# Delta-rule attention and a gated MLP on one Trainium2 core: a new list for the order of all instructions

## Chip, cores and metric

The kernel runs on one core of a Trainium2 chip. The metric is the device time of one execution in microseconds (us). The engines are TensorE (PE, matmuls), VectorE (DVE), ScalarE (ACT) and GpSimd (POOL); SyncE (SP) issues all bulk transfers.

## What is computed

The reference takes `q`, `k`, `v` (4 batches, 8 heads, 768 positions, 48 features) and `beta`, and runs a delta-rule attention over the positions; the result, reshaped to 4 x 768 x 384, goes through a gated MLP. `w_in` is 384 x 1024, `w_spatial` 768 x 768, `w_out` 512 x 384.

```python
k_n = k / (norm(k, axis=-1) + 1e-06)
state = zeros((B, H, D, D))
for t in range(S):
    y[t] = q[t] @ state
    v_old = state^T k_n[t]
    state += beta[t] * outer(k_n[t], v[t] - v_old)

h = relu(x @ w_in)                # x is y, heads side by side
u, v = h[..., :512], h[..., 512:]
v_n = (v - mean(v)) / sqrt(var(v) + 1e-06)
v_s = w_spatial @ v_n + b_spatial # over the positions
out = (u * v_s) @ w_out
```

## The kernel before, in words

**Attention.** The loop over 768 positions is done in chunks of 64. Twelve chunks for each of two pairs of batches make 24 steps `s`, and four steps make a group `g` (six groups). `prep(g)` (L476) makes the products of keys of its four steps (matmuls `kk`), copies them out, transposes them (L525), works out norms (L533 to L541) and scales the matrix `la` (L543). Then it inverts small unit triangular matrices one column at a time: each column is a product and a sum on DVE, a "lane". Group 0 uses 16 x 16 blocks and DVE alone (`lanes16`, L576 and L581); the later groups use 32 x 32 blocks, with some columns on DVE and the others on POOL (`lanes`, L563 and L568). ACT copies the DVE part out of PSUM (L586, L594), and one DVE transpose (L595) brings the result into `xt`. `widen16` (L655; group 0 only) and `widen` (L621) merge the blocks to 64 x 64 by matmuls: for a pair of steps, DVE transposes the diagonal blocks into `tn` (L625), PE does `e`, ACT scales its result into `tn` (L646), PE does `f`, and ACT copies that back (L651). `step(s)` (L730) then does the recurrence of one chunk: `v` minus the old state's part (L747 on DVE into `bn`), the product with the inverse, `w` (L777 on ACT), the state's update (L790, L792 on DVE), and the output (L807 on ACT). `scale_v` (L707) and the masked product of queries and keys (L724) stand ahead of it.

**Weights.** `w_in`, `w_spatial` and `w_out` arrive as raw 64-bit floats, and `load_f64` (L386) turns them into 32-bit ones with a chain over DVE (L392, L398, L400), ACT (L394 to L397, L401) and DVE or POOL (L402, L403). `split_w` (L382) splits each into a high part (ACT, L383) and a remainder (DVE or POOL, L384: `win_l`, `wsp_l`, `wout_l`), as each matmul of the MLP is three: high x high, high x remainder, remainder x high.

**Gated MLP.** After every second step `convert` (L817) brings 128 positions of two batches into the layout of the MLP and splits them (`xh` on ACT at L827, `xl` on DVE or POOL at L828); `mlp_v`, `norm_v`, `split_v` (L880) and `mlp_u` make the two halves of `h`, `mlp_g` (L948) does the products over positions and the gate (L962, L965, L967, L968), and `mlp_o` the last product and the store. Matmuls of all parts are recorded at one line, L453.

**Order.** Nothing is issued when these functions run. They record 2642 operations in a `Plan` (L167); an operation that can run on two or three engines has them listed in `alt`. `ORDER` (L36) is a list of words; each is four times the number of an operation plus the index of the engine that it takes. `Plan.issue` (L204) goes through the list, so the list sets the order on each engine and on SP's transfer queue, the choice of engine, and which buffer of a pool an operation gets:

```python
for i, sel in order:
    o = self.ops[i]
    for p, h in o.acq:
        h.unit = self.pools[p].pop(0)
    if o.fn is not None:
        e = list(o.alt)[sel]
        o.fn(e) if len(o.alt) > 1 else o.fn()
```

Of the kernel before, what the change touches and what calls it, by code (L numbers as in the profile page):

```python
# [36 lines left out]
12 0 28 52 64 4 40 448 8 928 24 32 56 36 68 60 44 936 88 85 1076 72 1064 49  # L37
80 96 93 292 20 16 1112 100 344 452 108 152 112 116 468 1080 120 124 456 128 132 136 1100 1084
160 140 608 460 148 1068 156 144 464 296 1088 1072 164 472 396 312 1692 500 168 476 300 932 172 348
480 1696 624 612 628 484 1104 176 304 489 76 180 184 2348 1108 188 552 352 192 1092 632 616 196 696  # L40
504 356 200 621 364 204 208 360 212 216 492 220 224 692 664 1096 400 2336 228 508 497 1732 232 236
308 240 104 244 1689 248 512 252 256 1729 404 260 264 268 516 1129 272 276 280 556 668 680 672 1125
284 684 677 408 1116 944 520 708 688 572 316 712 716 948 412 940 288 416 1000 952 560 320 524 1120
368 564 420 324 720 568 528 956 724 328 1004 728 576 736 372 988 424 532 1736 993 1008 969 732 1012
332 428 536 376 432 336 740 980 580 960 380 986 1060 966 744 996 1016 973 584 976 1640 1021 1028 541
1132 1040 1644 1048 1026 1045 1652 1648 588 1034 1656 1660 384 1136 1036 748 1140 1144 1668 1148 1664 752 388 1680
1700 1152 436 1156 1160 1704 756 440 1164 1708 592 1672 2340 1054 1168 1724 1712 1189 1056 596 1980 1740 2344 1172
1676 1716 1176 760 1684 1180 764 1984 544 392 636 1184 1720 2332 1196 1296 1200 445 1192 1748 1204 1744 1208 1752
1212 1216 1308 1220 1312 1224 2029 1756 1228 1992 1760 1232 1324 1236 1328 1768 1240 1776 601 1244 1248 1772 1252 1764
1988 1340 1796 2032 1256 341 1996 1260 1784 640 652 644 2000 1264 1800 2036 1344 2040 1792 1268 1356 2004 548 1788  # L50
2008 2016 2020 2048 1272 604 1360 2360 656 2044 1372 1780 1276 1376 2052 648 2056 1280 1388 700 1284 2068 661 1288
2060 2072 1292 2076 2064 1804 2352 1300 2092 704 2012 872 2081 1304 2356 2024 2384 1316 1808 2084 2372 1320 1392 2088
1404 1332 1408 2100 2096 1420 1836 1336 1424 1348 1436 1840 1352 1440 1916 1364 1452 2104 1368 876 1920 1380 1456 880
1384 1844 1468 2108 1396 1472 1400 2120 1484 1412 1924 1416 1488 2124 1428 1500 884 1432 2144 2376 1504 1444 892 1516
2112 1448 2140 2380 1460 1520 1464 2152 1532 888 1476 2364 1536 1480 2128 2400 896 1848 2136 2368 1492 2961 1928 1496
2132 2396 1508 1932 1512 1936 900 2148 1524 1852 1548 904 1528 2964 1552 3784 1540 1944 1544 1564 1940 1556 1568 2392
1560 1812 1580 1572 1576 1584 2116 1588 909 1856 2972 1592 2452 1816 913 1948 1952 916 2389 1956 2968 1820 1608 1621
2404 1628 3016 1601 1626 1960 1604 1964 1614 1632 1824 1968 1616 1636 2912 2408 921 1597 1828 3020 2916 2156 768 2412
3012 2920 2160 2924 1832 2928 2932 2416 2976 2164 2936 2420 2940 2168 2424 1972 2428 2952 772 2980 1976 2432 2948 2436
2984 2944 2440 2444 2172 2956 2988 776 2448 2992 2461 2456 2188 3432 780 3008 2568 2580 788 2192 2996 2584 784 2196  # L60
2596 2468 2472 2600 2200 2476 792 3024 2480 2612 2464 2484 3000 2616 2488 3028 2628 3436 3004 2632 2492 2496 2204 2644
2176 796 2500 2180 2648 2504 3032 2660 2184 2508 3036 1861 2512 2208 2664 2516 2268 2676 3040 2520 2300 2680 3440 2524
3044 2692 3444 2528 3052 1868 2696 3448 3060 3048 3452 2708 2532 3056 3492 2712 2536 1864 3481 3080 3484 2540 2544 3460
3064 2304 2213 3496 3468 2308 2724 3076 3456 2548 2272 2728 3488 3472 2276 3072 1873 1876 2740 2552 800 3084 3500 2744
2556 3504 3068 1880 2560 1885 2312 2756 2564 3796 3508 3533 2572 2280 2316 2576 2284 2588 2760 2320 2592 2772 2288 2604
2328 2776 3520 3088 2608 2788 3512 2620 1889 3524 2792 2624 3528 3093 2636 2324 3800 3516 2640 3544 3820 3804 2652 2216
2656 3536 3548 2804 3464 2668 3096 2808 3540 2296 3476 3100 2220 2672 3104 2684 1892 2688 2225 3552 1896 2228 2700 1900
2232 3556 2704 2237 2716 2820 3108 2292 2720 2824 3560 2732 3120 2241 2736 805 2748 3572 2752 2764 3112 3576 2768 3124
2836 2780 809 3116 2784 3584 3824 2796 2800 3588 3128 2812 3828 2840 2816 2828 3132 2852 3848 2832 2856 2844 3788 2848
2860 3564 812 3808 2864 3136 3792 3600 817 3200 3140 3204 3832 3208 3844 3212 820 3216 3596 3220 2900 2893 3812 3592  # L70
3900 2881 3232 3604 2872 2905 3236 3580 2897 2878 3240 2885 3244 2908 3816 3248 2888 4360 3252 3224 3841 3568 4364 3608
4409 4412 4368 4420 4372 3612 3228 4376 4380 3144 4416 3837 3720 4388 3724 4424 4384 2868 1904 3852 4400 4428 3256 4432
1909 4396 3728 4436 3732 3260 3152 4712 4440 4461 4448 3856 4456 4444 3752 4452 3860 3864 3756 3148 3868 3760 3872 3764
3156 3768 3876 3160 4392 3880 3772 3164 3884 4404 4464 3169 3776 3888 4472 3173 4468 3897 3736 4476 3740 4480 3748 3744
4484 2244 3892 3904 3616 4488 3908 3916 1912 4492 4500 3176 4760 3920 3780 4508 4016 3912 3924 4028 4496 4716 4032 3928
4044 3620 3932 3181 3936 3184 4048 3640 3940 2249 3644 4504 3648 824 4724 3944 4516 4060 3652 4720 3948 4064 4528 2252
3952 4728 4772 4076 3956 4080 4512 4764 3188 3960 4092 4732 6124 4096 4768 4524 3656 4108 4740 3624 3964 3193 4736 4776
4520 3628 2256 4752 3968 3632 6112 3972 4780 3636 4532 2260 4784 3976 4112 3264 4788 3980 4124 3268 3660 3984 4128 3272
3988 828 3276 4140 3992 3280 4144 832 3284 3996 4156 840 4800 4160 3288 4744 4792 4172 4804 3292 4176 4808 4796 4536
3296 4188 3300 4192 2264 3304 4813 4824 4748 836 4816 4756 4204 3308 844 3320 848 3324 4820 852 3328 3312 857 3332  # L80
3316 3336 3340 861 4828 3376 4000 4832 3344 3665 4836 3668 4208 4004 3348 4541 4852 4008 3672 3352 4012 3356 4840 4020
3380 4024 3360 6736 4844 4036 4220 3364 4040 3677 3384 3680 4224 4052 4848 3368 3684 4056 3388 4236 864 4864 3372 3392
3396 4876 3688 4068 3404 3693 3696 4872 3408 4072 4240 3400 3412 4252 4860 3416 3701 4084 3420 4256 4088 3424 4268 4100
# [1022 lines left out]
```

## Time and profile before

| | |
|---|---|
| median of 3 runs | 447.9 us |
| the runs | 447.9, 449.64, 447.23 us |
| profiled execution, span | 449.0 us |
| PE busy | 400.4 us (89%), 8648 matmuls |
| DVE busy | 282.0 us (63%), 692 instructions |
| ACT busy | 251.0 us (56%), 548 instructions |
| POOL busy | 177.9 us (40%), 352 instructions |
| bulk transfers | 41.27 MB in 15936 packets |
| program text fetched while it runs | 68 packets, 1.11 MB |

The profile gives one execution; its span is its own time, 1.1 us above the median and inside the range of the runs. Its chain of work that ended last goes through PE for 73%, DVE for 12%, ACT for 7%, transfers for 4% and for 3% through waits that nothing in the profile ends. "Idle before" stands for the time in which the engine did nothing ahead of an instruction, and behind the arrow is what ended it.

### The profile page before, as it was taken

How to read it: one execution, taken by the hardware profiler on the slowest of the kernel's cores; microseconds unless marked ns; L12 is line 12 of the kernel's file. 1: busy time of each engine (PE TensorE's matmuls, PEld its weight loads, DVE VectorE, ACT ScalarE, POOL GpSimd, SP SyncE). 2: the span in 40 equal slices, each digit the busy share in tenths (PEclk: the TensorE clock that was granted, in tenths of full speed). 3: DMA queues.
4: the chain of work that ended last, by engine and by line, in shares of the span. 5: the costliest groups of instructions: out<-in, count | busy, mean ns of one | idle time of the engine just before them, and what ended most of it. 6: DMA issues, size and time to landing. Idle time of an engine off the chain costs nothing.

```text
span 449.0 us, 19525 instructions
## 1 busy us (share of the span) xinstructions
PE 400.4 (89%) x8648; PEld 362.6 (81%) x8648; DVE 282.0 (63%) x692; ACT 251.0 (56%) x548; POOL 177.9 (40%) x352
## 2 busy tenths in 40 slices
PE   3414577889998999999999999999999999999996
PEld 3314577678788798879889889899889899999996
DVE  2889899898967669838898789824312323441330
ACT  4789864786676663877345874255435751430212
POOL 5162176838654845322784248540312100221121
PEclk9999999999999999999999999999999999999999
DMA  7951066324443423043241230132201000000102
GB/s 251 318 209 39 3 218 208 111 70 170 141 131 109 141 85 113 9 133 117 86 153 58 86 110 19 69 112 86 92 12 38 2 35 1 19 0 37 72 35 89
DMA packets 16020, 42.51 MB, mean 95 GB/s; under 512 B 3392, under 2 KB 7616, under 8 KB 15936
## 3 DMA queue, kind: packets, MB, share of 16 engines
q1 hardware_dynamic: 15936, 41.27, 27.3%
q8 instruction: 68, 1.11, 1.0%
q14 instruction: 16, 0.13, 0.1%
HBM read 35.36 MB, written 4.72 MB: 89 GB/s over the span
## 4 chain that ended last, share of the span: by engine, by line
PE 73%; DVE 12%; ACT 7%; DMA 4%; issue 3%; SPq 0%; POOL 0%; DVEq 0%; ACTq 0%
PE ps L453 73%; DVE prod L563 2%; DVE ps L568 2%; ACT xt L327 2%; DMA vf<-in_w_in 1%; DMA g<-in_w_out 1%; DMA ke<-in_k_t 1%; DVE xt L595 1%; DVE ut L398 1%; ACT xt L651 1%; DVE ps L581 1%; ACT w L777 1%; DVE prod L576 1%; ACT tn L646 1%; DVE ut L392 1%
## 5 line engine op out<-in xcount | busy, mean ns | idle before, releaser
L453 PE MATMUL ps<-wsp_h,vf 128*128 128x256 f32 x480 | 104.1, 286 | 0.0
L453 PEld LDWEIGHTS ps<-wsp_h,vf 128*128 128x128 f32 x480 | 80.7, 188 | 1.7 <-ACT ut L904 0.3
L453 PE MATMUL ps<-wsp_l,vf 128*128 128x256 f32 x240 | 67.5, 281 | 0.0
L568 DVE TENSOR_TENSOR ps<-ps,prod 128x60 f32<-128x60 f32 (+9 forms) x150 | 45.9, 306 | 3.9
L563 DVE TENSOR_TENSOR prod<-ps,la 128x60 f32<-128x60 f32 (+9 forms) x150 | 44.7, 298 | 4.0
L453 PEld LDWEIGHTS ps<-wsp_l,vf 128*128 128x128 f32 x240 | 45.2, 188 | 0.3
L962 DVE TENSOR_TENSOR gt<-ps,bbc 128x512 f32<-128x512 f32 x18 | 12.4, 690 | 43.6 <-PE ps L453 43.6
L568 POOL TENSOR_TENSOR wl<-wl,prod 128x36 f32<-128x36 f32 (+4 forms) x90 | 32.4, 360 | 5.8
L563 POOL TENSOR_TENSOR prod<-wl,la 128x36 f32<-128x36 f32 (+4 forms) x90 | 31.5, 350 | 5.7
L453 PE MATMUL ps<-wout_h,g 128*128 128x384 f32 x112 | 30.9, 339 | 0.0
L453 PE MATMUL ps<-ke 64*64 64x64 f32 x704 | 18.3, 253 | 11.2 <-DMA ke<-in_k_t 4.6
L453 PE MATMUL ps<-bn 64*64 64x64 f32 x832 | 20.2, 241 | 8.9 <-ACT xt L327 4.5
L453 PEld LDWEIGHTS ps<-ke 64*64 64x64 f32 x704 | 15.2, 161 | 15.1 <-ACT xt L327 5.8
L453 PEld LDWEIGHTS ps<-bn 64*64 64x64 f32 x832 | 16.7, 150 | 13.0 <-ACT xt L327 5.4
L965 POOL TENSOR_TENSOR gt<-gt,ut 128x512 f32<-128x512 f32 x9 | 11.6, 1287 | 34.3 <-DVE gt L962 23.7
L453 PE MATMUL ps<-wsp_h,bn 128*128 128x256 f32 x96 | 24.9, 282 | 0.0
L724 DVE TENSOR_TENSOR pt<-ps,masks 128x512 f32<-128x512 f32 x24 | 16.4, 682 | 13.5 <-PE ps L453 13.5
L967 ACT CAST xt<-gt 128x512 fp32r<-128x512 f32 x10 | 6.2, 620 | 32.2 <-DVE gt L965 21.2
L651 ACT COPY xt<-ps 32x256 f32<-32x256 f32 x48 | 17.5, 364 | 11.1 <-PE ps L453 10.5
L968 POOL TENSOR_TENSOR xt<-gt,xt 128x512 fp32r<-128x512 f32 x5 | 6.5, 1296 | 43.3 <-ACT xt L967 35.4
L967 ACT CAST g<-gt 128x512 fp32r<-128x512 f32 x14 | 8.5, 616 | 26.4 <-DVE gt L965 16.7
L327 POOL COPY xt<-xt 32x512 f32<-32x512 f32 (+1 forms) x22 | 13.7, 623 | 22.8 <-DVE xt L595 11.2
(193 smaller groups left out, 1114.9 us busy)
## 6 DMA issues: line engine op xcount, KB each, us to landing
bn<-in_bun SPq DMA_DIRECT2D x22, 896.0 KB, 4.8
ke<-in_k_t SPq DMA_DIRECT2D x22, 256.0 KB, 4.0
out<-ob SPq DMA_DIRECT2D x24, 192.0 KB, 1.9
vf<-in_w_in SPq DMA_DIRECT2D x6, 512.0 KB, 6.7
g<-in_w_sp SPq DMA_DIRECT2D x3, 768.0 KB, 5.6
g<-in_w_out SPq DMA_DIRECT2D x4, 384.0 KB, 3.2
bn<-in_bun SPq DMA_DIRECT2D x2, 640.0 KB, 7.5
xs<-xs SPq DMA_DIRECT2D x66, 16.0 KB, 2.9
```

The costliest lines, as they stand in the source:

```text
L327: (nc.scalar.copy if e == "ACT" else ENG[e].tensor_copy)(out=out_, in_=in_)
L392: P.add({"DVE": d}, lambda: nc.vector.tensor_scalar(out=eu(), in0=w1(), scalar1=20, scalar2=0x7FF, op0=ALU.logical_shift_right, op1=ALU.bi ...
L398: P.add({"DVE": dve_t(n)}, lambda: nc.vector.scalar_tensor_tensor(out=eu(), in0=w1(), scalar=0x80000000, in1=eu(), op0=ALU.bitwise_and, op ...
L453: nc.tensor.matmul(o, l, r, start=start, stop=stop)
L563: P.add({eng: cost}, lambda: e.tensor_tensor(out=dst if j == i0 else pt, in0=w[:, :n, j : j + 1].broadcast_to([128, n, m]), in1=la3[:, j, ...
L568: P.add({eng: cost}, lambda: e.tensor_tensor(out=dst, in0=dst, in1=pt, op=ALU.add), rd=[pk], wr=[key], due=due)
L651: P.add({"ACT": 0.46}, lambda r=i(a), f=f: nc.scalar.copy(out=v()[r, :, f, :], in_=pq4[r, :, f - 1, :]), rd=["pe0"], wr=[("fo", s + par, a ...
L724: P.add({"DVE": 0.69}, lambda: nc.vector.tensor_tensor(out=pv, in0=qv.rearrange("p d (c t) -> p d c t", t=64), in1=mask.unsqueeze(1).unsqu ...
L962: P.add({"DVE": 0.69}, lambda: nc.vector.tensor_tensor(out=gt(), in0=v3(bank(h.unit), 256), in1=v3(sums(p, half), 256) if p else bias(th), ...
L965: P.add(both(512), lambda e: ENG[e].tensor_mul(out=gt_[t.unit], in0=gt_[t.unit], in1=u_(uh)[:, half * 512 : half * 512 + 512]), rd=[("u", ...
L967: P.add({"ACT": 0.62}, lambda: nc.scalar.copy(out=gv(gg)[0][:, hs], in_=gt_[t.unit]), rd=[kk], wr=[("gh", b, th, half)], due=due + 6)
L968: P.add(both(512), lambda e: ENG[e].tensor_sub(out=gv(gg)[1][:, hs], in0=gt_[t.unit], in1=gv(gg)[0][:, hs]), rd=[kk, ("gh", b, th, half)], ...
```

## The change

Only the list `ORDER` is another one. It has the same 2642 operations, each once; 135 of them take another engine of their `alt`, and on average an operation stands 30 places from where it stood. The new list was found by a search in which fetches of program text are kept clear of bulk transfers. The table is written in 75 lines in place of 112, so every line behind it has a number lower by 37 (L384 is L347, L392 L355, L398 L361, L543 L506, L563 L526, L568 L531, L576 L539, L581 L544, L595 L558, L707 L670, L747 L710).

```diff
 ORDER = """
-12 0 28 52 64 4 40 448 8 928 24 32 56 36 68 60 44 936 88 85 1076 72 1064 49
...
+8 20 52 56 24 0 80 28 60 32 37 64 40 68 73 76 84 89 448 44 452 48 93 344 1076 292 1080 96 100 456 460 464 108 468 348 112
...
```

In the rows below numbers behind a name are those of buffers (`ut_270` and `vf_206` are a piece of `w_in` in decoding and as it arrived), and "x2" stands for two in a row.

DVE, at the start of the inverse of group 0, before. The lanes are the rows of L576 and L581:

```order
L543 TENSOR_TENSOR la<-la,dv 128x512 x2
L392 TENSOR_SCALAR ut_270<-vf_206 128x512
L576 TENSOR_TENSOR ps<-ps,la 128x2x15
L398 SCALAR_TENSOR_TENSOR ut_214<-vf_115,ut_214 128x512
L576 TENSOR_TENSOR prod<-ps,la 128x56
L400 TENSOR_SCALAR vf_115<-vf_115 128x512
L581 TENSOR_TENSOR ps<-ps,prod 128x2x2x14
L392 TENSOR_SCALAR ut_302<-vf_212 128x512
L724 TENSOR_TENSOR pt_72<-ps,masks 128x512
L402 TENSOR_TENSOR ut_214<-ut_214,vf_115 128x512
L576 TENSOR_TENSOR prod<-ps,la 128x78
```

Decodes of weights, a mask product and a sum of `ut` stand between the first lanes. The same place in the new order, where the lanes are L539 and L544:

```order
L506 TENSOR_TENSOR la<-la,dv 128x512 x2
L355 TENSOR_SCALAR ut_265<-vf_261 128x512
L539 TENSOR_TENSOR ps<-ps,la 128x2x15
L539 TENSOR_TENSOR prod<-ps,la 128x56
L544 TENSOR_TENSOR ps<-ps,prod 128x2x2x14
L539 TENSOR_TENSOR prod<-ps,la 128x78
L544 TENSOR_TENSOR ps<-ps,prod 128x2x3x13
L539 TENSOR_TENSOR prod<-ps,la 128x96
L544 TENSOR_TENSOR ps<-ps,prod 128x2x4x12
L539 TENSOR_TENSOR prod<-ps,la 128x110
```

The lanes now follow one another; the decodes stand ahead of the first and behind the last of them.

DVE, from the copy of the first state to the L747 of step 1 (buffer `bn_75`), before:

```order
L792 COPY s<-ps 112x384
L625 STREAM_TRANSPOSE tn_71<-xt_88 128x512
L543 TENSOR_TENSOR la<-la,dv 128x512 x2
L384 TENSOR_TENSOR wout_l<-g_493,wout_h 128x384
L384 TENSOR_TENSOR win_l<-ut_302,win_h 128x512
L563 TENSOR_TENSOR ps<-ps,la 128x31
L563 TENSOR_TENSOR prod<-ps,la 128x60
L553 STREAM_TRANSPOSE nn_97<-nl 128x32
L568 TENSOR_TENSOR ps<-ps,prod 128x2x30
L747 TENSOR_TENSOR bn_75<-bn_75,ps 128x384
```

Two remainders of weights and the transpose `tn` of the next pair stand between the state and `bn_75`. The same place in the new order:

```order
L755 COPY s<-ps 112x384
L366 TENSOR_TENSOR ut_232<-ut_232 128x512
L526 TENSOR_TENSOR ps<-ps,la 128x31
L526 TENSOR_TENSOR prod<-ps,la 128x60
L531 TENSOR_TENSOR ps<-ps,prod 128x2x30
L526 TENSOR_TENSOR prod<-ps,la 128x87
L531 TENSOR_TENSOR ps<-ps,prod 128x3x29
L526 TENSOR_TENSOR prod<-ps,la 128x112
L531 TENSOR_TENSOR ps<-ps,prod 128x4x28
L526 TENSOR_TENSOR prod<-ps,la 128x135
L531 TENSOR_TENSOR ps<-ps,prod 128x5x27
L710 TENSOR_TENSOR bn_75<-bn_75,ps 128x384
```

The two remainders are gone from it, `la` is scaled ahead of the state copy, and nine lanes of group 1 stand where three stood.

POOL, in the lanes of group 1, before:

```order
L563 TENSOR_TENSOR wl<-wl,la 128x19
L384 TENSOR_TENSOR win_l<-ut_373,win_h 128x512
L563 TENSOR_TENSOR prod_69<-wl,la 128x36
L568 TENSOR_TENSOR wl<-wl,prod_69 128x2x18
L707 TENSOR_TENSOR bn_74<-bn_74,nn_96 128x384
L563 TENSOR_TENSOR prod_69<-wl,la 128x51
L568 TENSOR_TENSOR wl<-wl,prod_69 128x3x17
L384 TENSOR_TENSOR win_l<-ut_416,win_h 128x512
L563 TENSOR_TENSOR prod_69<-wl,la 128x64
L384 TENSOR_TENSOR win_l<-ut_270,win_h 128x512
L568 TENSOR_TENSOR wl<-wl,prod_69 128x4x16
```

Three `win_l` stand between the first lanes. A later piece of the same lanes in the new order, where two of the products are ones that DVE did before:

```order
L670 TENSOR_TENSOR bn_74<-bn_74,nn_96 128x384
L531 TENSOR_TENSOR wl<-wl,prod_69 128x6x14
L347 TENSOR_TENSOR win_l<-ut_225,win_h 128x512
L526 TENSOR_TENSOR prod_69<-wl,la 128x91
L531 TENSOR_TENSOR wl<-wl,prod_69 128x7x13
L526 TENSOR_TENSOR prod_69<-wl,la 128x96
L347 TENSOR_TENSOR win_l<-ut_232,win_h 128x512
L531 TENSOR_TENSOR wl<-wl,prod_69 128x8x12
L347 TENSOR_TENSOR win_l<-ut_360,win_h 128x512
L526 TENSOR_TENSOR prod_69<-wl,la 128x99
L347 TENSOR_TENSOR win_l<-ut_355,win_h 128x512
```

The products are further into the lanes, and there are more of them: `win_l` of five pieces and an `ut` product stand between lanes now.

## Rows read from the trace of the kernel before

**Rows 1.** Busy time by stretch: us, PE, PEld, DVE, ACT, POOL, granted clock, DMA share, GB/s
```profile
0.00:48.52 48.52, 17.76 (x833) 15.63 (x833) 35.87 (x82) 38.13 (x67) 17.10 (x43) 1.00 0.56 189
48.52:77.71 29.19, 22.00 (x801) 19.61 (x801) 26.27 (x63) 17.26 (x38) 16.16 (x26) 1.00 0.47 153
77.71:97.44 19.73, 16.84 (x413) 13.49 (x407) 17.89 (x48) 14.60 (x30) 13.38 (x29) 1.00 0.35 118
97.44:240.00 142.56, 138.79 (x3570) 120.70 (x3569) 110.80 (x308) 90.21 (x209) 77.82 (x172) 1.00 0.34 111
240.00:445.54 205.54, 205.03 (x3044) 193.20 (x3042) 91.16 (x196) 90.28 (x204) 53.44 (x84) 1.00 0.15 51
```

**Rows 2.** Timeline of PE: start, us, instruction, count [idle before, releaser]
```profile
48.52 1.49 PE L453 MATMUL ps<-tn,xt 32*32 32x32 f32 x64 [1.15 <-DVE tn L625]
...
77.71 0.97 PE L453 MATMUL ps<-win_h,xh 128*128 128x512 f32 x3
...
96.29 0.91 PE L453 MATMUL ps<-xt,tn 64*64 64x64 f32 x24 [1.03 <-ACT tn L646]
...
136.14 1.15 PE L453 MATMUL ps<-xt,tn 64*64 64x64 f32 x32 [1.19 <-ACT tn L646]
```

**Rows 3.** Timeline of DVE, 16 to 91 us
```profile
16.10 0.19 DVE L576 TENSOR_TENSOR ps<-ps,la 128x30 f32<-128x30 f32 x1
...
23.27 2.06 DVE L392 TENSOR_SCALAR ut<-vf 128x512 uint32<-128x512 uint32 x1 [1.36 <-DMA vf<-in_w_in]
...
32.12 2.11 DVE L595 STREAM_TRANSPOSE xt<-wl 128x1024 f32<-128x1024 f32 x1 [0.33 <-ACT wl L586]
34.09 1.50 DVE L384 TENSOR_TENSOR wsp_l<-g,wsp_h 128x768 fp32r<-128x768 f32 x1
...
47.76 0.70 DVE L625 STREAM_TRANSPOSE tn<-xt 128x512 f32<-128x512 f32 x1
...
59.04 1.52 DVE L384 TENSOR_TENSOR wout_l<-g,wout_h 128x384 fp32r<-128x384 f32 x1 [0.21 <-ACT wout_h L383]
...
88.89 2.20 DVE L595 STREAM_TRANSPOSE xt<-wl 128x1024 f32<-128x1024 f32 x1 [0.23 <-ACT wl L594]
```

**Rows 4.** Groups of DVE instructions, 15.75 to 32.1 us: count, busy, mean ns, idle before
```profile
L392 DVE TENSOR_SCALAR ut<-vf 128x512 uint32<-128x512 uint32 x5 | 3.8, 761 | 1.4 <-DMA vf<-in_w_in 1.4
L581 DVE TENSOR_TENSOR ps<-ps,prod 128x56 f32<-128x56 f32 (+7 forms) x14 | 3.6, 258 | 0.3
L576 DVE TENSOR_TENSOR prod<-ps,la 128x56 f32<-128x56 f32 (+7 forms) x14 | 3.6, 255 | 0.4
L384 DVE TENSOR_TENSOR wsp_l<-g,wsp_h 128x768 fp32r<-128x768 f32 x1 | 1.0, 959 | 0.3 <-ACT wsp_h L383 0.3
```

**Rows 5.** Timeline of POOL beside the DVE row at 23.27 us
```profile
23.24 1.81 POOL L384 TENSOR_TENSOR wsp_l<-g,wsp_h 128x768 fp32r<-128x768 f32 x1 [2.89 <-ACT wsp_h L383]
```

**Rows 6.** Timeline of POOL: first and last lane of group 1
```profile
58.38 0.54 POOL L563 TENSOR_TENSOR wl<-wl,la 128x19 f32<-128x19 f32 x1 [8.48 <-DVE la L543]
...
86.15 0.46 POOL L568 TENSOR_TENSOR wl<-wl,prod 128x19 f32<-128x19 f32 x1
```

**Rows 7.** Groups of POOL instructions, 58.38 to 86.61 us
```profile
L384 POOL TENSOR_TENSOR win_l<-ut,win_h 128x512 fp32r<-128x512 f32 x3 | 3.8, 1269 | 0.0
L707 POOL TENSOR_TENSOR bn<-bn,nn 128x384 f32<-128x384 f32 x3 | 2.5, 834 | 0.5 <-DMA bn<-in_bun 0.5
L384 POOL TENSOR_TENSOR wsp_l<-g,wsp_h 128x768 fp32r<-128x768 f32 x1 | 2.3, 2267 | 3.1 <-ACT wsp_h L383 3.1
```

**Rows 8.** Waits of PE with nothing to release them: us, times, longest; one of them
```profile
PE ps L453 <- issue: 3.1, 4, 1.5
...
152.78 0.26 PE L453 MATMUL ps<-s,bn 64*64 64x48 f32 x2 [0.53 <-issue]
```

**Rows 9.** Groups of the gate's second product on POOL and on DVE
```profile
L965 POOL TENSOR_TENSOR gt<-gt,ut 128x512 f32<-128x512 f32 x9 | 11.6, 1287 | 34.3 <-DVE gt L962 23.7 <-DVE st L865 9.0 <-DVE ps L568 1.6
...
L965 DVE TENSOR_TENSOR gt<-gt,ut 128x512 f32<-128x512 f32 x15 | 10.3, 689 | 0.5
```

183 rows, old and new, of the table ORDER are left out of this document.

## Prediction

> **What bounds the kernel now.** I read the busy times by stretch first. From 97.44 us on TensorE (PE) is busy for 138.79 of 142.56 us and then for 205.03 of 205.54 us; ahead of it, it is busy for 17.76 of 48.52, 22.00 of 29.19 and 16.84 of 19.73 us [rows 1]. So 40.8 us of its idle time lie in the first 97 us, 4.3 in the next 348. Its work stays as it is: the same matmuls on the same engine, at a granted clock of 1.00 in every stretch [rows 1]. The end can therefore move by what is saved or lost in the idle time ahead of 97 us, and by little else unless another engine makes PE wait later.
>
> The second view is PE's timeline: who ends its waits [rows 2]. Its first level merge (`e`, 64 matmuls) starts at 48.52 behind the vector engine's (DVE) transpose `tn`; the first matmul of the gated part starts at 77.71; the block `f` of the second inverse group starts at 96.29 behind an ACT copy of `tn`. Behind that only short waits are left, the longest 1.19 us at 136.14.
>
> The third is DVE's timeline of that stretch [rows 3]. The triangular inverse of group 0 runs as 29 small DVE lanes (L576, L581) from 16.10 us to the transpose L595 at 32.12; `tn` follows at 47.76. Group 1 runs on DVE and on GpSimd (POOL) and ends in its own L595 at 88.89. So `f` at 96.29 hangs on a chain of DVE: inverse 0, `tn`, norms, inverse 1. In 29.2 and 19.7 us of the two middle stretches DVE is busy 26.3 and 17.9 [rows 1]: here its order is the time.
>
> **The change, part by part.** *Inverse 0.* From 16.10 to 32.12 are 16.0 us. The lanes in it are 3.6 + 3.6 us [rows 4] plus the first, 0.19 [rows 3]: 7.4 us. Between them stand decodes of weights (L392, 5 of 0.76, with 1.4 us waited for the load of `w_in`), L398, L400, L402, the mask product L724, and `wsp_l` (0.96, 0.3 waited) [rows 4]. One L392 took 2.06 us beside a POOL product of 1.81 that started 0.03 us earlier [rows 3, 5]; the four others of that row are left with 0.44 each. In the new order one L724 alone stands between lanes, at 0.6 to 0.7 us. With a tenth of a microsecond or less between neighbours I take 8.4 us for 29 lanes. Ahead of them the new order puts three L392 with an L398 and two L400 where one or two L392 stood: they start 1.6 us later, at 17.7. Two L392 (0.35 each) come before the transpose, beside ACT's copy. 17.7 + 8.4 + 0.6 + 0.7 is 27.4, or 27.5: the transpose is 4.6 us earlier. The bound below comes from the SP queue: the third `w_in` piece, which the lanes now stand behind, may land late by up to the 1.4 us that such a piece was waited for [rows 4]; so 3.1 to 4.6.
>
> *From that transpose to `tn`.* The new order adds `wsp_l` (0.96) and an L398 and L400s there, and takes out an L662 half, an L400 and an L392, as well as the 0.54 that `wsp_l` lost at 34.09 beside POOL (1.50 for 0.96) [rows 3, 4]. I count it 0.3 to 0.8 worse, up to 2 if the late decodes wait for loads: `tn` comes 2.0 to 4.1, about 3.4 us earlier than 47.76.
>
> *From `tn` to the gated part.* `wout_l` (1.52 at 59.04, beside POOL [rows 3]) and a `win_l` go to POOL, the next pair's `tn` (0.7) goes behind, and L747, which makes `bn` for the next step, is no longer behind them. An L403 (0.7) and six more lanes (1.6) come ahead of it instead. I take about 1.0 us more: the first gated matmul some 4.4 earlier than 77.71. This costs PE nothing of itself; it is given back unless `f` also comes earlier, since the same 68 groups of matmuls stand ahead of `f` in both orders.
>
> *Inverse 1* decides. DVE is busy for 80.0 us before 97.44 [rows 1]. With every instruction that either order lists ahead of this L595 at the duration that its line has in the trace, 78.6 us stand there before and 72.9 now; so the DVE side ends 5.7 earlier at most. POOL takes over: two `win_l` and an `ut` product at 1.27 each and a `wout_l` of three quarters of that size, about 1.0, less one `bn` product of that size, 0.9: 3.9 us more in its lanes [rows 7]. They ran from 58.38 to 86.61 [rows 6], 28.2 us. They would start at about 54 (3.4 from `tn`, 1.0 of the 2 us by which L543 moves ahead of the state copy), and end at 54 + 28.2 + 3.9 = 86.1, or at 83.0 if the 3.1 us that POOL waited there for `wsp_h` goes, as that product stands late in the new order. The transpose needs both sides: it comes at 83.2 (DVE alone) to 86.1, which is 5.7 to 2.8 earlier. I take **4.0**, near the middle. `f` follows it as before, so PE's idle time ahead of 97 us falls by 4.0.
>
> *Fetches of program text.* The change moves them off bulk loads. PE's waits with nothing to release them are 3.1 us in all, four times [rows 8]. The one at 152.78 (0.53) falls beside bulk loads; the other three, 2.6 us, lie between 37 and 46 us, inside the long bursts of 16x16 matmuls of the first widening, with no bulk load under way. There DVE's chain sets the pace. So this part is worth 0 to 0.5 us; I count 0. If all four waits went and PE kept what it gained, it would be 3.1 us and the sum 440.8. The Trainium skill (Runtime: NRT & Kernel Launch, "Instruction fetch mechanics") says of crossing a block of program text that it is mostly hidden; by that the part is worth nothing and the sum is as I have it, though the waits of [rows 8] show that it is not always hidden.
>
> *Behind 97 us.* DVE has less work ahead of each later point (its whole work falls by some 12 us), POOL has 21 more, ACT the same. PE is 97 to 99.8% busy [rows 1]; the 4.3 us that are left could shrink or grow. I count 0, and minus 1.5 to plus 1.5 for the range. The tail behind 445.54 (last copy and store, 3.5 us) stays.
>
> **Sum:** -4.0. The profiled execution's span is 449.0 us, 1.1 above the median of 447.9 and inside 447.23 to 449.64; against it the sum gives 445.0, against the median **443.9 us**.
>
> **Rivals.**
> *No change (447 to 449).* DVE and POOL give the gain back: inverse 1's POOL part ends as late as before (the 3.9 us, and no wait saved, and a start of 56), or PE, early by 4 us, runs into waits that were hidden until now: those like the 1.19 at 136.14 [rows 2] grow until they have taken back 4 us. For it: these waits sit on inverse 2 and on the state chain, which have work of their own. Against: DVE has less to do before each of them. Chance 0.22.
>
> *POOL becomes the bound (about 451.5), slower.* The place is the stretch behind 97 us, where the new order gives POOL gate products and four 128x768 `xl` remainders that DVE did. A gate product takes 1.29 us on POOL, 0.69 on DVE [rows 9]; a 128x768 remainder 1.81, against 0.96 on DVE [rows 4, 5]. Four `xl` at 0.85 and seven gate products at 0.60 are 7.6 us more. POOL is busy for 77.8 of 142.6 us and 53.4 of 205.5 there [rows 1], so they find room unless PE needs each at once. If it waits for all of them, 447.9 - 4.0 + 7.6 = 451.5; the rival decides once PE's waits for POOL are over 4 us. Against it: none of PE's waits in the profile names POOL. Chance 0.13. DVE slows beside POOL too, as the L392 of 2.06 us did [rows 3]. The Trainium skill (SBUF — State Buffer, "Who interferes with whom") says that the two share a pair of ports, and that whoever issues first holds it for its whole instruction while the other waits. The trace agrees: 2.06 is near the sum of the product's 1.81 and the decode's own 0.44 [rows 3, 5]. By that rule 21 us more of POOL, at DVE's share of 282 in 449 us, could stop DVE for up to 13 us; if PE waited for half of that the time would be 450.4, between this rival and no change.
>
> **How the numbers follow.** The forecast has 0.65: the inverse chain is seen in rows, and both bounds of it are gains. The low end adds to the full DVE gain of 5.7 the 1.5 us and the 0.5 of the fetches: 447.9 - 7.7 = 440.2, so 440.0. The high end is the no-change case with a little of its spread: 448.4; the slower rival is mostly left out. A measurement of this kernel tells about 0.5% from no change, 2.2 us: faster means under 445.7, slower over 450.1. The forecast's own spread (440 to 445) gives 0.65 for faster, no change 0.22, the POOL rival 0.13 for slower.
>
> **What would show it.** In the new profile `tn` of group 0 should start at about 44.4, the first gated matmul at about 73.3, L595 of group 1 at about 84.9, the `f` group near 92.3; PE's idle time ahead of it should be near 36.8 us instead of 40.8, and the stretches behind it 97 to 99.8% busy. The step on inverse 0 is wrong if its transpose comes later than 29; the step on inverse 1 if POOL's last lane ends after 87; the count of 0 behind 97 us if PE idles there by over 6 us, or if its waits name L828, L965 or L968 on POOL. Were fetches the real gain, PE's and DVE's waits with no releaser would vanish and the time would fall without the transposes moving.

## Result, and the profile after

The changed kernel is faster: the ratio to the kernel before is 0.9905 (95% interval 0.9879 to 0.9932), 4.3 us of 448.0. The medians of the 20 runs of each are 445.3 and 448.02 us; the ratio leaves disturbed runs out and the medians do not, so the two numbers differ. Runs of one kernel spread over 2.2% after (439.8 to 449.4) and 1.3% before (445.7 to 451.6).

Busy time by stretch of the changed kernel, cut at the first `e`, at the first gated matmul, behind `f` of step 4 and at the end of PE's work (columns as in [rows 1]):

```profile
0.00:43.02 43.02, 16.37 (x800) 14.39 (x800) 32.49 (x79) 35.57 (x64) 17.79 (x42) 0.64 0.62 217
43.02:67.98 24.96, 19.22 (x801) 17.43 (x801) 23.46 (x61) 18.45 (x42) 16.80 (x31) 0.74 0.45 152
67.98:86.55 18.57, 16.80 (x445) 13.93 (x439) 16.15 (x44) 12.18 (x27) 14.13 (x27) 1.00 0.41 134
86.55:240.00 153.45, 146.08 (x3680) 128.25 (x3680) 119.01 (x322) 98.36 (x224) 86.02 (x176) 0.99 0.33 108
240.00:438.24 198.24, 197.22 (x2933) 187.03 (x2931) 82.70 (x184) 84.21 (x192) 61.42 (x87) 1.00 0.15 50
```

The granted clocks of the first two stretches cannot be set against [rows 1]: the profile of the kernel before holds no record of the clock ahead of 71.4 us, and the view shows time without a record as 1.00. The account of the prediction comes back to it.

Against [rows 1] the first three stretches are 86.55 us long in place of 97.44, and PE is idle for 34.2 of them in place of 40.8. But in the fourth PE is now idle for 7.4 of 153 us, where it was 3.8 of 143. PE's timeline of the same kernel, at the places of [rows 2], and two waits that are new (a count below 32 or 64 is a group that the end of the view cuts off, its start is whole):

```profile
43.02 1.05 PE L416 MATMUL ps<-tn,xt 32*32 32x32 f32 x59 [1.15 <-DVE tn L588]
...
85.40 0.80 PE L416 MATMUL ps<-xt,tn 64*64 64x64 f32 x20
...
96.77 0.44 PE L416 MATMUL ps<-pt,w 64*48 64x64 f32 x16 [3.06 <-issue]
...
128.35 0.69 PE L416 MATMUL ps<-ke 64*64 64x64 f32 x32 [2.06 <-DMA ke<-in_k_t]
```

`e` is 5.5 us earlier than in [rows 2] and `f` of step 4 is 10.9 us earlier. Then PE waits 3.06 us that nothing in the profile releases, and 2.06 us for a load of keys. DVE's timeline, as in [rows 3]:

```profile
16.48 0.19 DVE L539 TENSOR_TENSOR ps<-ps,la 128x30 f32<-128x30 f32 x1
...
26.12 2.13 DVE L558 STREAM_TRANSPOSE xt<-wl 128x1024 f32<-128x1024 f32 x1
...
42.26 0.70 DVE L588 STREAM_TRANSPOSE tn<-xt 128x512 f32<-128x512 f32 x1
...
77.76 2.22 DVE L558 STREAM_TRANSPOSE xt<-wl 128x1024 f32<-128x1024 f32 x1 [0.95 <-POOL wl L531]
```

Inverse 0 now takes 9.6 us from its first lane to its transpose, in place of 16.0. The transpose of inverse 1 ends a wait for POOL. POOL's timeline and its groups in the lanes of group 1, as in [rows 6, 7]:

```profile
50.94 0.35 POOL L526 TENSOR_TENSOR wl<-wl,la 128x19 f32<-128x19 f32 x1 [3.55 <-ACT ps L514]
...
77.48 0.24 POOL L531 TENSOR_TENSOR wl<-wl,prod 128x19 f32<-128x19 f32 x1
...
L347 POOL TENSOR_TENSOR win_l<-ut,win_h 128x512 fp32r<-128x512 f32 x5 | 6.4, 1274 | 0.0
L347 POOL TENSOR_TENSOR wsp_l<-g,wsp_h 128x768 fp32r<-128x768 f32 x1 | 1.8, 1822 | 0.0
```

The lanes run for 26.8 us (28.2 before) though five `win_l` stand in them in place of three: the `wsp_l` there no longer waits for ACT, nor is it slowed. POOL is now on the chain of work that ended last, for 10% of the span in place of 0.

One profile of each kernel is one execution, so a second was taken of both. Added up from PE's timeline (idle is the sum of gaps between matmuls):

| us | before | before, 2nd | after | after, 2nd |
|---|---|---|---|---|
| span | 449.0 | 447.7 | 442.3 | 442.6 |
| PE idle ahead of `f` of step 4 | 40.8 | 40.5 | 34.2 | 32.6 |
| PE busy | 400.4 | 399.1 | 395.7 | 396.8 |
| PE idle from `f` to its last matmul | 4.2 | 4.5 | 8.4 | 9.4 |
| tail | 3.5 | 3.6 | 4.1 | 3.8 |

In the means the span falls by 5.9 us: 7.3 of idle time ahead of `f`, 3.5 of busy time (all of it ahead of `f`), less 4.5 more idle behind `f` and 0.4 in the tail. That is more than the 4.3 of the ratio, as these are two executions of each kernel and the ratio is of twenty.

### The profile page after: what moved, and what is told of

Its sections match the earlier page's. It is cut to its first block, busy times and chain, and to the rows that moved or that the text cites. A ratio compares the mean times of both kernels' runs of the same rounds, so it can differ in the third digit from the quotient of the medians.

```text
span 442.3 us, 19529 instructions
## 1 busy us (share of the span) xinstructions
PE 395.7 (89%) x8648; PEld 361.0 (82%) x8648; DVE 273.8 (62%) x686; ACT 249.2 (56%) x545; POOL 196.2 (44%) x360
## 4 chain that ended last, share of the span: by engine, by line
PE 64%; DVE 11%; POOL 10%; ACT 5%; issue 4%; DMA 3%; SPq 1%; ACTq 0%; POOLq 0%; DVEq 0%
PE ps L416 64%; POOL prod L526 2%; POOL wl L531 2%; DVE ps L531 2%; DVE prod L526 2%; SPq L311 1%; POOL win_l L347 1%; POOL xt L290 1%; DMA bn<-in_bun 1%; DVE xt L558 1%; DVE ps L544 1%; POOL wsp_l L347 1%; DVE prod L539 1%; DMA bn<-in_k_t 1%; DVE tn L588 1%
## 5 line engine op out<-in xcount | busy, mean ns | idle before, releaser
L416 PE MATMUL ps<-wsp_h,vf 128*128 128x256 f32 x480 | 99.8, 285 | 0.0
L416 PEld LDWEIGHTS ps<-wsp_h,vf 128*128 128x128 f32 x480 | 79.0, 188 | 1.3
L531 DVE TENSOR_TENSOR ps<-ps,prod 128x60 f32<-128x60 f32 (+9 forms) x150 | 45.9, 306 | 4.1
L526 DVE TENSOR_TENSOR prod<-ps,la 128x60 f32<-128x60 f32 (+9 forms) x150 | 44.7, 298 | 4.0
L526 POOL TENSOR_TENSOR prod<-wl,la 128x36 f32<-128x36 f32 (+4 forms) x90 | 32.1, 357 | 6.1
L531 POOL TENSOR_TENSOR wl<-wl,prod 128x36 f32<-128x36 f32 (+4 forms) x90 | 32.1, 356 | 5.9
L740 ACT COPY w<-ps 128x384 f32<-128x384 f32 x24 | 11.5, 478 | 38.3 <-PE ps L416 38.2
L416 PE MATMUL ps<-wout_h,g 128*128 128x384 f32 x112 | 31.8, 342 | 0.7 <-ACT vr L814 0.7
L928 POOL TENSOR_TENSOR gt<-gt,ut 128x512 f32<-128x512 f32 x12 | 15.7, 1320 | 34.7 <-DVE gt L925 34.7
L416 PEld LDWEIGHTS ps<-ke 64*64 64x64 f32 x704 | 14.9, 158 | 18.3 <-issue 3.9
L290 POOL COPY xt<-xt 32x512 f32<-32x512 f32 (+1 forms) x23 | 14.1, 614 | 26.8 <-DVE xt L558 12.3
L770 ACT COPY xs<-ps 112x512 f32<-112x512 f32 x24 | 14.0, 585 | 16.9 <-PE ps L416 16.7
L416 PE MATMUL ps<-wsp_h,bn 128*128 128x256 f32 x96 | 23.3, 281 | 0.0
L416 PE MATMUL ps<-xh,win_h 128*128 128x256 f32 x120 | 22.6, 297 | 0.0
L753 DVE TENSOR_TENSOR s<-s,ps 112x384 f32<-112x384 f32 x20 | 11.0, 548 | 18.0 <-PE ps L416 17.7
```

The lines of the kernel that those rows point to most:

```text
L290: (nc.scalar.copy if e == "ACT" else ENG[e].tensor_copy)(out=out_, in_=in_)
L416: nc.tensor.matmul(o, l, r, start=start, stop=stop)
L526: P.add({eng: cost}, lambda: e.tensor_tensor(out=dst if j == i0 else pt, in0=w[:, :n, j : j + 1].broadcast_to([128, n, m]), in1=la3[:, j, ...
L531: P.add({eng: cost}, lambda: e.tensor_tensor(out=dst, in0=dst, in1=pt, op=ALU.add), rd=[pk], wr=[key], due=due)
L740: P.add({"ACT": 0.48}, lambda: nc.scalar.copy(out=v3(w, 192), in_=v3(pc, 512)[:, :, 0:192]), rd=["pc"], wr=[("w", s % 2)], due=due + 2)
L753: P.add({"DVE": 0.55}, lambda: nc.vector.tensor_tensor(out=sv, in0=sv, in1=pv, op=ALU.add), rd=["pc"], wr=["S"], due=due + 3.2)
```

## Experiments

Each time is given as a ratio to the kernel before, measured beside it (its median there was 448.2, 449.0 or 449.6 us); times 448 it compares with what was expected.

**Second profiles.** No edit.

> The changed kernel once more, for a second profile. If the two profiles compared so far show what belongs to the order, the transposes of inverses 0 and 1 start again within 0.5 us of 26.1 and 77.8, groups of 32 small matmuls again fall from about 1.1 to 0.7 us near 53 us, PE's idle time up to its last matmul is again near 42.5 us, and the 3.1 us wait with no releaser at 96.8 us and the 2.1 us wait for a load of ke at 128 us come back. If these are chances of one execution, the time at which small matmuls become fast moves by over 5 us, or one of the two waits is gone and the span differs by 2 us or more.

> The kernel before once more, for a second profile. If its slow small matmuls (groups of 32 at 1.1 us until 71 us) belong to its order, they end again at 69 to 73 us, PE is busy for 400 us and idle for 45. If the first profile was a late one by chance, its span of 449.0 falls to about 446 and the small matmuls become fast earlier, with PE's busy time nearer to 396.

The table above has the spans. The transposes, the idle time ahead of `f` and the pace of small matmuls came back; the two long waits did not. PE's waits in the second profile of the changed kernel, and PE at the place where the first had lost 3.06 us:

```profile
PE ps L416 <- DMA bn<-in_bun: 4.0, 2, 2.8
...
PE ps L416 <- issue: 3.0, 5, 1.7
...
92.38 0.63 PE L416 MATMUL ps<-pt,w 64*48 64x64 f32 x32
```

The 32 matmuls `pt,w` now ran through in 0.63 us, and 2.8 us went into a load of `bn` at 157 us instead. So the front's gain belongs to the list; behind `f` some 4 us are lost in both executions, but not at the same place. The wait of 3.06 us is no chance of one execution, though: a wait of 2.87 to 3.08 us at the same place of PE's program, its instruction 4523, stands in the profiles of back_new, slow_inverse0 and new_order_old_engines below.

**Half of the list.** Lists that begin as the one and go on as the other:

```diff
-order = new
+front_new: new up to f of step 4 (516 operations), then the others as in before
+back_new:  before up to f of step 4 (535), then the others as in new
+front_126: new for 830 operations, then the others as in before
```

> The new list up to the matmuls f of step 4 (515 operations, some 86 us), then all others in the sequence and on the engines of the list before. If the gain is made on the chain inverse 0, tn, inverse 1, it is all here: f of step 4 near 85.4 us, and the time is that of the changed kernel or better by up to 4 us, as the two long waits behind 90 us belong to the new list's later part: 441 to 445. If the gain comes from where fetches of program text fall over the whole program, this mixed list, which nobody placed, keeps at most half: 446.5 or more.

> The old list up to f of step 4 (534 operations), then the rest in the sequence and on the engines of the new list. If the gain lies in the front, this is no faster than before, 447.5 to 452, with f of step 4 at 95 to 97 us and PE idle some 4 us more behind it. If the gain comes from the later part (fetches clear of transfers, work moved to POOL), it is 444 to 446.

> The new list for its first 830 operations (to about 126 us), then the rest in the sequence and on the engines of the list before; at this point the two lists have done nearly the same operations (18 differ), so that little is left over to be done at the seam. If the gain lies in the chain inverse 0, tn, inverse 1 and the 7 us wait of the first mixed list was its seam alone (it ended with a left-over chain of decodes), this keeps it: 442 to 446. If a new front is worth nothing without the list that was found together with it, 448 or more, with a long wait of PE again right behind 126 us.

Measured: front_new 1.0029 (1.0002 to 1.0056), back_new 1.0107 (1.0072 to 1.0141), front_126 0.9972 (0.9933 to 1.0011). PE in the three:

```profile
86.03 1.15 PE L452 MATMUL ps<-xt,tn 64*64 64x64 f32 x32
94.17 1.22 PE L452 MATMUL ps<-win_h,xh 128*128 128x512 f32 x2 [6.99 <-ACT vr L850]
...
107.76 0.54 PE L452 MATMUL ps<-pt,w 64*48 64x64 f32 x12 [2.87 <-issue]
...
85.18 1.03 PE L452 MATMUL ps<-xt,tn 64*64 64x64 f32 x28
```

With the new front `f` comes at 86.03 and 85.18, 10 and 11 us early: this gain needs no later part. In front_new PE then waits 7 us for a bank that ACT has not read out, as ACT and DVE work through a left-over decode of `w_out` at the seam; the gain is gone at once. front_126 has a cleaner seam and a profiled execution of 442.9 us, but that is the fastest of its runs, which spread from 444.9 to 453.4, and the interval of its ratio reaches 1; whether it keeps the gain was not settled. The old front with the new rest is slower than either list. In none of the three was the gain of the new front kept for certain by a rest that was not found with it.

**The lanes of inverse 0 alone.** In the list before, four decodes (13 operations with what hangs on them) move from between the lanes to behind the transposes L662; DVE's order:

```diff
-L402 TENSOR_TENSOR ut_214    (between lanes)
-L392 TENSOR_SCALAR x3        (between lanes)
 L595 STREAM_TRANSPOSE xt_88
 L662 STREAM_TRANSPOSE la x2
+L402 TENSOR_TENSOR ut_214
+L392 TENSOR_SCALAR x3
```

> The list before, with one thing of the change alone: three L392 and one L402 (with what hangs on them) no longer stand between the lanes of inverse 0 but behind the second transpose L662. The transpose L595 should start 4 to 5 us earlier, at 27 to 28. If inverse 0 sets the time of all that follows, tn of step 0 and f of step 4 come 3 to 4 us earlier and the time is 444 to 446. If the decodes only change places, ahead of tn instead of ahead of L595, tn gains under 2 us and the time is 446.5 to 449.

Measured: 1.0097 (1.0064 to 1.0129). DVE's timeline, then PE's:

```profile
28.65 2.00 DVE L594 STREAM_TRANSPOSE xt<-wl 128x1024 f32<-128x1024 f32 x1 [0.65 <-ACT wl L585]
...
41.43 2.06 DVE L397 SCALAR_TENSOR_TENSOR ut<-vf,ut 128x512 uint32<-128x512 uint32 x3 [2.33 <-ACT ut L395]
...
52.73 0.71 DVE L624 STREAM_TRANSPOSE tn<-xt 128x512 f32<-128x512 f32 x1
...
44.48 0.70 PE L452 MATMUL ps<-xt,bbc 32*16 32x16 f32 x62 [6.91 <-DVE xt L684]
...
100.94 1.15 PE L452 MATMUL ps<-xt,tn 64*64 64x64 f32 x32 [1.03 <-ACT tn L645]
```

The transpose L594 (L595 before) starts 3.5 us earlier, and yet `tn` starts at 52.73, 5.0 later than in [rows 3], `f` of step 4 at 100.94 (4.65 later), and the kernel loses 4.3 us. The decodes that were put off need ACT in their middle: L397 at 41.43 waits for it, the L684 that PE needs stands behind that, and PE waits 6.91 us. Neither of the expected cases held. What passes on to the end is the time of `tn`, not that of the transpose: 5.0 us there were 4.3 in the ratio.

**The lanes made slower.** In the changed kernel:

```diff
-nc.vector.tensor_tensor(out=dst if j == 0 else pt, ...)
+[nc.vector.tensor_tensor(out=dst if j == 0 else pt, ...) for _ in range(2 if j else 1)]
```

> The changed kernel with each of the 14 products of the lanes of group 0 done twice, to the same result: 3.6 us more of DVE ahead of L595. If the chain through inverse 0 sets the end, L595 starts near 29.7, f of step 4 is 2.5 to 3.6 us later than 85.4 and the time 447 to 449. If there is slack (DVE waits 2.2 us for PE ahead of tn, and PE waits for loads later), under 1 us of it is seen: 444.5 to 446.

Measured: 0.9983 (0.9951 to 1.0015), 3.5 us above the changed kernel's 0.9905.

```profile
30.50 2.12 DVE L558 STREAM_TRANSPOSE xt<-wl 128x1024 f32<-128x1024 f32 x1
...
88.41 0.80 PE L416 MATMUL ps<-xt,tn 64*64 64x64 f32 x20
```

The transpose is 4.4 later, `f` of step 4 3.0 later, the end 3.5 (by intervals of 0.3% each): little or no slack. DVE's chain through inverse 0 still sets the end of the changed kernel.

**Old engines.** The sequence of the new list, the engine of each operation from the list before:

```diff
-[(op, engine in new) for op in new]
+[(op, engine in before) for op in new]
```

> The sequence of the new list with the engine choices of the list before (135 operations go back, by which POOL loses some 18 us and DVE gains 8 to 12). If the gain is in the sequence alone and POOL's share only costs, 442 to 445. If the two belong together, DVE is late on the chain to inverse 1 (79 us of work instead of 73 ahead of its transpose), f of step 4 comes 2 us or more later than 85.4 and the time is 446 to 450.

Measured: 1.0424 (1.0377 to 1.0470), the slowest of all. Its profile is of the slowest of its runs (475.8 us, the others took 467.3 to 470.4):

```profile
89.39 2.17 DVE L594 STREAM_TRANSPOSE xt<-wl 128x1024 f32<-128x1024 f32 x1 [1.65 <-ACT wl L593]
...
98.26 1.94 PE L452 MATMUL ps<-xt,tn 64*64 64x64 f32 x32
...
PE ps L452 <- DMA ke<-in_k_t: 10.7, 4, 3.5
PE ps L452 <- issue: 9.6, 9, 3.1
```

Inverse 1 ends at 89.39 again, as it did before the change, and `f` comes at 98.26, 12.9 late against the changed kernel. So the new sequence needs its engines, the products that went from DVE to POOL among them. How much of the rest of the loss is the engines' own was not separated: in this execution 10.7 us went into loads of keys and 9.6 into waits that nothing releases, with PE's instructions in the order of the changed kernel.

**More work for PE where it waits.** To the changed kernel, at nine places between 14 and 56 us:

```diff
+def warm():
+    for c in range(2):
+        mm(bank(7)[:, c * 128 : c * 128 + 128], masks[:, 0:128], masks[:, 0:128])
```

> The changed kernel with 36 matmuls of 128x128 by 128 columns more, whose result nobody reads, at the places between 14 and 56 us where PE waits. If the small matmuls are slow (groups of 32 at 1.1 us) because PE does little ahead of them, they fall to 0.7 us at 20 to 30 us in place of 53, PE's time in the groups up to 53 us falls by 3 to 5 us, and the time is 441 to 443.5. If PE's share of work has nothing to do with it, they stay at 1.1 until about 53 us and the time is 445 to 447.

Measured: 1.0105 (1.0058 to 1.0152).

```profile
22.23 0.69 PE L453 MATMUL ps<-bn 64*64 64x64 f32 x32 [1.82 <-ACT xt L327]
...
26.24 0.69 PE L453 MATMUL ps<-ke 64*64 64x64 f32 x32 [1.79 <-DVE pt L724]
...
48.09 1.13 PE L453 MATMUL ps<-bn 64*64 64x64 f32 x32
...
20.00:30.00 10.00, 5.11 (x120) 4.27 (x118) 9.15 (x29) 9.61 (x17) 6.17 (x7) 1.00 0.62 233
30.00:50.00 20.00, 14.92 (x656) 13.15 (x658) 16.11 (x29) 17.00 (x34) 4.30 (x8) 0.57 0.22 71
...
PE ps L453 <- issue: 13.6, 11, 2.8
```

The small groups did become fast, 0.69 us at 22 and 26 us; then the granted clock fell (0.57 in the mean of 30 to 50 us: 0.50, the level of 1.2 GHz, for most of it), with PE busy for 14.9 of those 20 us, and a group took 1.13 again. But the kernel came out 9 us slower than the changed one, with 13.6 us of waits that nothing releases, where that has 3.0 to 6.5. The added matmuls (72, each with a weight load, so 144 instructions) had moved PE's program text. Three kernels measured that by itself.

**Program text moved.** One operation of small matmuls before PE's gap (36 or 64 calls; in the changed kernel ahead of the `kq` at 19.75 us, in the kernel before ahead of the first widening):

```diff
+def pad():
+    for c in range(36):
+        mm(bank(7)[0:64, c % 4 * 64 : c % 4 * 64 + 64], masks[0:64, 0:64], masks[0:64, 64:128])
```

> The changed kernel with 36 small matmuls of 64x64 more (72 instructions of PE, about 1 us), whose result nobody reads, put where PE idles for 5.4 us near 15 to 20 us; so every later block of PE's program text begins 72 instructions earlier in the work. If waits for program text depend on where a block's fetch falls among bulk loads, and the new list was found for its own positions, the sum of PE's waits with no releaser rises from 4 to 6.5 us to over 9 and the time is 447 to 453, though the work hides in idle time. If only the order of the work counts, the time is that of the changed kernel within its spread, 444 to 446.5.

> As the one before with 64 small matmuls (128 instructions, 1.7 us, still inside the 5.4 us gap): another position of the blocks. Positions count: a time that differs from the changed kernel and from the one before by 2 us or more, most likely above 447, as no search placed it. Order alone counts: 444 to 447 again.

> The kernel before with the same 36 small matmuls, in its gap of 7.2 us ahead of the first widening at 34 us. If both lists were found for their own positions, it loses as the changed kernel does, by 2 to 6 us: 450 to 454, with more fetches late behind loads. If the list before was blind to fetches, its positions are as good as any, and the time stays within 1.5 us of 448.

The expectations counted wrong: each such call is two matmuls with a weight load each, so the pads are 144 and 256 instructions, and they took 7.9 and 13.9 us. PE's groups of the pad, waits with no releaser and `f` of step 4, in after_pad72, after_pad128 and before_pad72:

```profile
L452 PE MATMUL ps<-masks 64*64 64x64 f32 x72 | 7.9, 311 | 0.0
...
PE ps L452 <- issue: 18.3, 15, 3.3
...
91.52 1.15 PE L452 MATMUL ps<-xt,tn 64*64 64x64 f32 x32
...
L452 PE MATMUL ps<-masks 64*64 64x64 f32 x128 | 13.9, 311 | 0.0
...
PE ps L452 <- issue: 4.5, 6, 1.8
...
92.10 1.11 PE L452 MATMUL ps<-xt,tn 64*64 64x64 f32 x31
...
PE ps L452 <- issue: 13.4, 14, 1.5
...
96.42 0.80 PE L452 MATMUL ps<-xt,tn 64*64 64x64 f32 x20 [1.03 <-ACT tn L645]
```

Measured: after_pad72 1.0127 (1.0085 to 1.0169), after_pad128 0.9996 (0.9953 to 1.0039), before_pad72 1.0265 (1.0220 to 1.0311). The count that was wrong makes a better test. 17,296 matmuls and weight loads (2 x 8648) came in 68 packets of 16 KB, about 254 a packet: a pad of 256 instructions moves the text by one whole block, so that each block begins at the work where one began before; a pad of 144 does not. And the pad of 256, though longer, leaves 4.5 us of waits with no releaser and costs 0.9% against the changed kernel; the pad of 144 has 18.3 us of them and costs 2.2%, with `f` at nearly the same time in both. This comparison is weaker than it looks: the 11 runs of after_pad128 spread from 447.1 to 457.1 us, its profile is of the fastest of them, and five lie among those of after_pad72 (453.9 to 457.7). By the medians of all runs (453.4 and 456.1) the two pads cost 1.5% and 2.1%. The clear case is the kernel before. There the pad lies in idle time (`f` at 96.42, as in [rows 2]), and 144 instructions cost 2.65%, 12 us, and the waits with no releaser grow by 10.3 (13.4 in place of 3.1).

Where those waits fall is a count. Numbers of the instruction that waits, among PE's matmuls and weight loads, in after_pad72:

```
953 1209 1465 1719 2229 2741 4779 5035 5799 7329 9625 10135 12175 14473 15239
```

The steps are 256, or multiples of it less 1 or 2 in 256. PE's 66 semaphore and drain instructions stand in the text too; with them counted, all 91 waits with no releaser in the fourteen profiles of this case begin at place 193 or 194 of a block of 256. warm_pe, which adds 144 instructions as well, has its eleven at eleven of the fifteen numbers above. So each is the start of a block. In the trace a block's packet starts a while after PE has begun the block ahead of it, and the block's first instruction ran 1.0 to 1.6 us after the packet's end wherever PE waited for it. That while is 0.7 to 1.0 us in the median where under 50 KB of bulk loads moved in it; where more did, 1.2 to 1.5, and 2.3 and 2.5 in the two short pads. Of some 60 blocks up to 330 us, it was over 2 us for 7 and 8 in the two profiles of the kernel before, for 2 and 2 in those of the changed one, and for 16, 3 and 14 in after_pad72, after_pad128 and before_pad72. It was 4.3 us ahead of the wait of 3.06 us at 96.77. A late packet need not cost anything: lanes_together has 8 of them and no such wait. Bulk loads in that stretch (40 slices of 0.25 us from 88 to 98 us):

```profile
DMA  0000000000000993789898992200000000000003
GB/s 0 0 0 0 0 0 0 0 0 0 0 0 0 201 229 57 287 344 401 373 430 344 401 459 115 94 0 0 0 0 0 0 0 0 0 0 0 0 0 66
```

0.91 MB moved from 91 to 94.3 us, and the packet started at 94.34. That a block's packet stands behind the loads is what these starts suggest; no run moved the loads and left the text alone.

## Why the prediction was right

The forecast was 443.9 us in a range of 440.0 to 448.4, faster with 0.65; the ratio stands for 443.7 and the median is 445.3. The sign and the place held: the chain of inverse 0, `tn` and inverse 1 came earlier, and slow_inverse0 shows that the end hangs on it. That the size came out as well is in part luck. Ahead of `f` some 10.8 us were gained where 4.0 were forecast, and behind it 4.9 were lost where 0 was forecast (means of the two profiles of each); two terms left at 0 are of 3 to 5 us and of opposite sign.

*Inverse 0* was forecast at 27.5 and 3.1 to 4.6 earlier; it started at 26.12, 6.0 earlier. The lanes began at 16.48 and not at 17.7 as counted: from the transpose of `la` ahead of them to the first lane it took 0.8 us more and not 1.6, and that transpose started 0.45 earlier (9.56 in place of 10.01). From the first lane on the 9.8 us counted were 9.6.

*To `tn`* was forecast as 0.3 to 0.8 worse, up to 2. From the transpose to `tn` it took 16.1 us in place of 15.6: the sum of the row differences held (0.5). `tn` came 5.5 earlier (3.4 forecast, 4.1 at most; the two ranges that it was added up from give 1.1 to 4.3).

*The first gated matmul* came at 67.98, 9.7 earlier than 77.71, where 4.4 were forecast; as the prediction says, this alone saves PE nothing.

*Inverse 1* was forecast 2.8 to 5.7 earlier, 4.0 taken; it was 11.1 earlier. This term was the most mis-sized. Two steps of POOL's side failed. The first is the start of its lanes at about 54: they began at 50.94, as `tn` came 5.5 earlier and not 3.4, and the way from `tn` to the first lane fell by 1.9 (10.6 to 8.7) and not by 1.0. The second is their length. 3.9 us more was right as work (4.1 in the rows), but 4.0 us of waits went (the 3.1 for `wsp_h` and 0.5 for a load among them) and `wsp_l` and the lanes ran some 1.1 faster, so that the length was 26.8 and not 32.1. The bound of 5.7 for DVE's side failed too: DVE's busy time ahead of this transpose fell by 7.7 (71.7 to 64.0), and its idle time, which the bound held fixed, by 3.4 (17.2 to 13.8). That POOL would be the side that ends last was right: the transpose waited 0.95 us for it.

*PE's idle time ahead of `f`* was to fall by 4.0, as far as `f` came earlier, and fell by 6.6 (7.3 in the means), while `f` came 10.9 earlier. The equality failed because PE's busy time ahead of `f` fell too, by 4.2 and 2.5 us in the two profiles, with the same matmuls. The prediction put that at nothing, on the reading that the granted clock is 1.00 in every stretch [rows 1]. This reading is wrong: the first profile's record of the clock begins at 71.4 us. The second profile of the kernel before has the record from 7.8 us on: the clock is at 0.50, its level of 1.2 GHz, until 69.2 us but for two short spells, and at 1.00 from there. In the changed kernel it rises at 52.7 and, after one more fall, for good at 59.6. Group `ke` of 32 and the clock around it, kernel before (second profile), then changed kernel (columns of the clock's rows: us, PE busy, granted clock, DMA share, GB/s):

```profile
55.19 1.09 PE L453 MATMUL ps<-ke 64*64 64x64 f32 x32
62.50:69.10 6.60, 5.71 (x184) 0.50 0.75 266
69.30:97.00 27.70, 22.23 (x646) 1.00 0.41 132
72.26 0.69 PE L453 MATMUL ps<-ke 64*64 64x64 f32 x32 [0.35 <-ACT xs L807]
...
43.00:52.60 9.60, 8.07 (x268) 0.50 0.07 11
49.48 1.12 PE L416 MATMUL ps<-ke 64*64 64x64 f32 x32
59.70:86.50 26.80, 22.69 (x749) 1.00 0.44 146
65.58 0.69 PE L416 MATMUL ps<-ke 64*64 64x64 f32 x32 [0.35 <-ACT xs L770]
```

So the busy time fell because the higher level came earlier, with the same kinds of group at 0.7 us in place of 1.1. Why it came earlier is only in part known. Seven profiles record the rise and add no work to PE: the second of the kernel before, both of the changed one, front_new, front_126, slow_inverse0 and new_order_old_engines. In them an earlier `e` goes with an earlier first rise behind it, in the same order throughout (`e` at 42.1 to 47.6 us, the rise at 51.4 to 59.0). So this gain came together with that of `tn`; that the one brings the other was not tested, and warm_pe, which had the higher level at 22 us, lost it again.

*Behind 97 us* 0 was counted, with 1.5 either way. It was 4.5 us of idle time. Of POOL's 18 us more of work PE felt nothing directly, as no wait of PE names POOL. It went into waits for loads (the 2.06 at 128 us in one execution, 2.8 at 157 in the other) and for program text. The test that the prediction set, idle time there of over 6 us, gave 8.4 and 9.4: by it, the count of 0 was wrong.

*Fetches* were counted 0. As a gain that was right: the waits with no releaser are 3.1 and 2.7 us before, 6.5 and 3.0 after. The change does what it says, since blocks fetched late fell from 7 and 8 to 2 and 2, but those that are left cost as much or more. The 3.1 us bound what could be won; they say nothing of what a list can lose: the list before with its text moved by 144 instructions pays 12 us, and the changed one pays 5.9 us more for 144 than for a whole block (1.0127 less 0.9996; 2.7 by the medians of all runs). The Trainium skill (Runtime: NRT & Kernel Launch, "Instruction fetch mechanics") says that crossing a block is mostly hidden. The two lists as they stand agree: 3 to 6.5 us for 68 blocks. The padded ones do not, where 128 small matmuls (0.63 to 1.15 us for 32) use a block up in 2.5 to 4.6 us: 18.3 us in 15 waits were not hidden.

*The rivals.* No change and POOL as the bound did not come as a whole. The lost 4.5 us are of the first one's kind (PE, early, meets waits that were hidden), with loads and text in place of ACT's copies.

## What to carry to other kernels

Follow the one value that the next engine needs (`tn` here) and not the end of the stage that looks long: bringing inverse 0 forward by 3.5 us made the kernel 4.3 us slower, since the work that was put off came due ahead of `tn`. A list of instructions, its engines and its tail were one object here: the two halves of the better list came out 0.3% and 1.1% above the old one, and its sequence without its engines 4.2%. Before a granted clock of 1.00 is believed, look whether the profile holds a record of it there; the durations of one kind of group tell the level too. Where an engine runs hundreds of short instructions, any edit that adds or removes some of them moves all later blocks of program text; before a small change is believed, measure the same kernel with the text padded by part of a block.

## What had not been expected

Padding PE's text by 144 instructions of no use costs 2.65% in one list and 2.2% in the other, more than twice what the change brings; a whole block of 256 costs 0.9% with twice the pad (1.5% by the medians).

The pace of small matmuls follows the granted clock wherever the profile has a record of it: in the fourteen profiles the 42 groups `ke` and `bn` of 32 that lie at 0.50 took 1.09 to 1.14 us, and the 464 at 1.00 took 0.66 to 0.85. A 1.00 with such groups at 1.1 us, as in [rows 1] ahead of 71.4 us, was time without a record.

Two long waits of PE behind `f` cost more than their own length. After the 3.06 us at 96.77 the granted clock was 0.50 from 97.2 to 100 us with PE busy throughout, and so it was from 157.5 to 160.5 in the second profile, after the 2.8 us for `bn`. The profile of the kernel before is at 1.00 from 71.4 us to the end of PE's work.

Why the runs of one kernel spread so differently was not settled. The waits for text in one profile do not tell it: after_pad72, with 18.3 us of them, stayed within 453.9 to 457.7, front_126, with 2.0, spread over 444.9 to 453.4, and lanes_together, with none, stayed within 453.2 to 455.3.
